# Last batch of an attention and feed-forward kernel: its dense layers by seven block products, with the output feature-major, and a planner with other margins and due times

## The chip, the cores and the metric

One core of a Trainium2 chip runs the whole program. The metric is the device time of one execution in microseconds; three executions of the kernel before gave 443.0, 445.16 and 446.7 us, and their median, 445.16 us, is the time before. Line numbers such as L659 are lines of the kernel before; those of the changed kernel are given as such.

## What is computed

Four batches of 768 tokens, eight heads of 64 features. The first half is an attention in a window of 32 tokens, to which 24 block summaries (maximum of k, mean of v over 32 tokens) are added as further keys. Its output `x` (768 tokens by 512 features a batch) goes through a feed-forward part with a gate. All is float32:

```python
    x_prev = np.concatenate([np.zeros((B, 1, D), dtype=np.float32), x[:, :-1, :]], axis=1)
    xk = mu_k * x + (1.0 - mu_k) * x_prev
    xr = mu_r * x + (1.0 - mu_r) * x_prev
    k = np.maximum(xk @ w_k, 0.0)              # 512 -> 1024
    v = k * k @ w_v                            # 1024 -> 512
    r = 1.0 / (1.0 + np.exp(-(xr @ w_r)))      # 512 -> 512
    return (r * v).astype(np.float32)
```

## The kernel before

**How the work is tiled.** The tokens go through the dense layers in eight halves of 384 tokens (four batches, two halves each; below, half 0 to half 7). For a half there are three blocks of PE work. The gate `gate_tile` (L586) takes three tiles of 128 tokens by 512 features and multiplies by `w_r`. `experts` (L616) runs over eight slices `j` of 128 of the 1024 hidden features: `first(j)` (L621) makes a slice of `k` with features on partitions and 384 tokens wide (L632), ACT squares its positive part (L639, L641), and `second(j)` (L651) multiplies the slice by `w_v` and adds it into three banks of PSUM, tokens on partitions and 512 features wide (L659). DVE multiplies by the gate (L689) and SP stores (L693).

**Precision.** A float32 operand is split into a rounded part (`kh`, `xh`, `w_h`) and its rest (`kl`, `xl`, `w_l`), both in a format that PE takes in one pass. A product is three matmuls: high by high, high by low, low by high. So a `first(j)` is 4 x 3 = 12 matmuls of 128x384, a `second(j)` 9 of 128x512, a gate tile 12 of 128x512. The splits are a cast (L573, L645, L646) and a subtraction (L575, L647) on ACT and DVE. In half 0, where the weights have only just come, the first slices run "plain", on unsplit float32, which PE takes in several passes: `PLAIN = 6, 6` says that six of the eight slices do, in both layers.

**Attention.** A batch has eight units (`unit`, L441): four pairs of heads, two halves of the tokens. A unit goes: scores on PE (L462), mask and row minimum on DVE (L473), exponential on ACT (L477), the factor 1/sum on DVE (L483, L484), normalisation on POOL (L489), a transposition in blocks on DVE (L514, "flip"), four transfers to DRAM ("put", L523) and one back ("get", L527) that finish the transposition, the product with the values on PE (L536), and a copy out of PSUM (L549, L547). The means of v reach the value tile by a transfer that copies them to each window ("spread", L436). All transfers are issued by SP, in one queue.

**What sets the order.** The program is written as a list of operations with costs and due times, and `Plan.schedule` (L145) lays them out: it goes forward in a time of its own, gives each engine the ready operation with the earliest start and due time, and emits the instructions in the order found. Each engine then runs its instructions strictly in that order and waits where data is missing. The table `LENGTH` (L39) has an assumed cost for each operation; a transfer is assumed to take `DMA_FIXED` plus its bytes. `LOCKS` (L70) lists the DVE operations during which the planner keeps POOL idle, and the reverse. Attention of batch b+1 is spread over the two halves before it: unit number n of a batch is due `UNITS` times (7 - n) before the last (L740). The last two halves, 6 and 7, have no attention beside them.

**Buffers.** Forty slots `w` of 128x512 hold the weights: high and low parts of 4 tiles of `w_r`, 8 of `w_k`, 8 of `w_v`.

Of the kernel before, what the change touches and what calls it, by code (L numbers as in the profile page):

```python
# [20 lines left out]
P = 128  # L21
# [23 lines left out]
    norm=345, wcast_p=640, mixa_p=600, kcopy_p=450, evac_a=375, flip=560,  # L45
# [20 lines left out]
ISSUES = dict(put=720, get=400, spread=820)  # L66
# [6 lines left out]
UNITS = 8500  # L73
# [26 lines left out]


class Op:
    def __init__(self, n, ways, due, bufs, size):
        self.n, self.ways, self.due, self.bufs, self.size = n, ways, due, bufs, size
        self.deps, self.succ, self.start, self.finish, self.eng = set(), [], None, None, None


class Plan:
    def __init__(self, pools, later):
        self.pools, self.later, self.ops, self.count = pools, later, [], {p: 0 for p in pools}  # L110
        self.writers, self.readers = {}, {}

    def buf(self, pool, dtype=F32, in_turn=True):
        n = self.count[pool] if in_turn else None
        self.count[pool] += in_turn
        return Buf(pool, n, dtype)
# [28 lines left out]
    def schedule(self):  # L145
# [7 lines left out]
        for o in reversed(self.ops):  # L153
            own = 1.0e9 if o.due is None else o.due
            wait = DMA_FIXED + o.size * DMA_NS_PER_BYTE if "SP" in o.ways else min(c for c, _ in o.ways.values()) + SLACK
            o.due = min([own] + [s.due - wait for s in o.succ])
        waiting = {o: len(o.deps) for o in self.ops}
# [17 lines left out]
        while any(ready.values()):  # L175
            best = None
            for e, now in engines.items():
# [3 lines left out]
                for o, at in ready[e]:  # L181
# [5 lines left out]
                    start, need, ok = max(at, now, o.due - EARLY if e == "SP" and o.name not in ("put", "get") else 0), {}, True  # L187
                    if e == "SP":
                        start = max(start, lanes[-LANES])
                    for x in o.bufs:  # L190
                        if x.place is None:
# [4 lines left out]
                            start = max(start, free_slots[x.pool][k][0])  # L196
# [23 lines left out]
            for x in o.bufs:  # L220
                if x.place is None:
                    _, x.place = free_slots[x.pool].pop(0)
                    turn[x.pool] += x.n is not None
# [16 lines left out]
            for x in o.bufs:  # L240
                x.left -= 1
                if not x.left:
                    end = max(u.finish + LATENCY[u.eng] for u in x.users)
                    pool, places = self.later.get(x.pool, (x.pool, [x.place]))
                    free_slots[pool].extend((end, place) for place in places)
                    free_slots[pool].sort(key=lambda s: s[0])
# [9 lines left out]
def tile_kernel(ctx: ExitStack, tc: tile.TileContext, q, k, vT, v, mask, ident, pool, sel, mu, w_k, w_v, w_r, out):  # L256
# [7 lines left out]
    def slots(name, n, shape):  # L264
# [3 lines left out]
    last_z = Slot(const, "z4", [P, 2, DM], "kt3")  # L268
    pools = dict(
        ktx=[last_kt], w=slots("w", 2 * (NCK + 2 * NCV), [P, 512]),  # L270
        kt=tiles("kt", 3, [P, KL]), qt=tiles("qt", 4, [P, HT]), vx=tiles("vx", 12, [P, S + 1]),
        kg=tiles("kg", 2, [P, 49]), ks=tiles("ks", 2, [P, NS]),
        vs=tiles("vs", 1, [P, NS]), vm=tiles("vm", 3, [P, P]), sp=tiles("sp", 2, [P, P]),
        y=tiles("y", 4, [P, NSL, P]), mn=tiles("mn", 4, [P, NSL]), sm=tiles("sm", 3, [P, 2 * NSL]),
# [564 lines left out]
```

## Time and profile before

| | us |
|---|---|
| runs | 443.0, 445.16, 446.7 |
| the profiled execution, its own time | 446.4 |
| its span, first to last instruction | 444.6 |
| PE busy | 433.3 (97%) |
| DVE busy | 274.5 (62%) |
| ACT busy | 269.1 (61%) |
| POOL busy | 109.4 (25%) |
| mean granted clock of PE | 0.995 |

How to read it: a row of the page or of a view names line, engine, operation, what it writes and reads, how often, and the time. The 1.8 us between the span and the execution's own time lie around the first and last instruction. A busy PE is not PE at its peak: matmuls overlap, so durations of single ones (0.40 us) are longer than the distance from one to the next, and the costs used below are distances between starts. A plain float32 matmul is two records in the trace.

The execution falls into a start of some 44 us, in which inputs arrive and the attention of batch 0 runs; half 0 with the weights arriving (to about 98 us); halves 1 to 5 with the attention of the next batch beside them, about 50 us each (to 354 us); halves 6 and 7 alone (354 to 441 us); and the last stores.

### The profile page before, as it was taken

The page shows a single profiled execution, that of the slowest core. Times are in us where ns is not written, and L with a number is a line of the kernel's source. Part 1 is how long each engine was busy: PE and PEld are TensorE (multiplying, and loading weights), DVE is VectorE, ACT ScalarE, POOL GpSimd, SP SyncE. Part 2 cuts the span into 40 slices and gives each one's busy share as a digit, 9 for nine tenths or more (in the row PEclk, how much of TensorE's full clock was granted, in tenths as well). Part 3 has the DMA queues.
Part 4 walks back from the last instruction along what each step waited for, and adds up shares of the span by engine and source line. Part 5 has one row for each costly group of instructions (what it writes and reads, how often), then busy time and mean ns, then how long its engine had stood idle before and what let it go on. Part 6 is the DMA issues. An engine that isn't in the chain of part 4 may idle for free.

```text
span 444.6 us, 9448 instructions
## 1 busy us (share of the span) xinstructions
PE 433.3 (97%) x3366; PEld 351.4 (79%) x3366; DVE 274.5 (62%) x890; ACT 269.1 (61%) x772; POOL 109.4 (25%) x245
## 2 busy tenths in 40 slices
PE   8998999997999999999999999999999999999996
PEld 8754555685888888887888888887888888888895
DVE  3798999897775658549474649559464444232213
ACT  3699989987855448558665459548665444232220
POOL 0692514672241005132150005232150001000000
PEclk9999999998999999999999999999999999999999
DMA  8968878677767243676647152867642010001001
GB/s 289 404 205 299 300 258 262 210 206 190 255 184 235 103 142 110 192 260 186 164 108 234 41 204 76 267 191 200 189 116 72 1 72 0 0 2 71 1 0 71
DMA packets 41509, 70.82 MB, mean 159 GB/s; under 512 B 4855, under 2 KB 24951, under 8 KB 41463
## 3 DMA queue, kind: packets, MB, share of 16 engines
q1 hardware_dynamic: 41463, 70.23, 49.5%
q8 instruction: 26, 0.43, 0.4%
q14 instruction: 20, 0.16, 0.1%
HBM read 52.71 MB, written 15.73 MB: 154 GB/s over the span
## 4 chain that ended last, share of the span: by engine, by line
PE 80%; DMA 9%; ACT 6%; DVE 3%; issue 1%; SPq 0%; ACTq 0%
PE mm L659 28%; PE mm L632 27%; PE av L536 5%; PE mm L593 4%; PE mm L595 4%; PE mm L594 4%; PE sc L462 4%; DMA st<-in_w_k 2%; ACT y L477 2%; DMA kt<-in_k 2%; PE mm L606 2%; DMA mu_sb<-in_mu 1%; DMA vx<-in_v 1%; DMA qt<-in_q 1%; ACT wc L328 1%
## 5 line engine op out<-in xcount | busy, mean ns | idle before, releaser
L632 PE MATMUL mm<-xs,w 128*128 128x384 f32 x744 | 149.1, 349 | 0.0
L632 PEld LDWEIGHTS mm<-xs,w 128*128 128x128 f32 x744 | 130.8, 188 | 10.5 <-issue 1.9
L489 POOL TENSOR_SCALAR y<-y,rc 128x120 f32<-128x120 f32 x192 | 85.4, 462 | 139.8 <-DVE rc L484 109.7
L659 PE MATMUL mm<-w,kh 128*128 128x512 f32 x348 | 94.6, 400 | 0.4 <-ACT kh L646 0.4
L477 ACT ACTIVATE y<-y,mn 128x120 f32<-128x120 f32 x192 | 73.4, 384 | 19.5 <-DVE mn L473 19.2
L639 ACT ACTIVATE r<-mm 128x384 f32<-128x384 f32 x64 | 31.1, 486 | 88.0 <-PE mm L632 87.9
L659 PEld LDWEIGHTS mm<-w,kh 128*128 128x128 f32 x348 | 64.3, 189 | 13.1 <-ACT kh L646 0.7
L645 DVE CAST kh<-r 128x384 fp32r<-128x384 f32 x41 | 15.4, 375 | 69.8 <-ACT r L641 69.7
L659 PE MATMUL mm<-w,kl 128*128 128x512 f32 x174 | 54.4, 406 | 0.0
L575 DVE TENSOR_TENSOR xs<-xa,xs 128x384 fp32r<-128x384 f32 x56 | 30.2, 554 | 31.2 <-ACT xs L573 31.1
L473 DVE CUSTOM_DVE_ANT_0 y<-sc,mask_sb 128x120 f32<-128x120 f32 x192 | 42.0, 275 | 5.4 <-PE sc L462 5.3
L561 POOL TENSOR_SCALAR xa<-vx,om_sb 128x384 f32<-128x384 f32 x16 | 12.4, 785 | 105.3 <-DVE xs L575 102.2
L659 PEld LDWEIGHTS mm<-w,kl 128*128 128x128 f32 x174 | 31.6, 189 | 7.6 <-DVE kl L647 0.5
L647 DVE TENSOR_TENSOR kl<-r,kh 128x384 fp32r<-128x384 f32 x58 | 32.7, 564 | 7.2 <-ACT kh L646 4.4
L536 PEld LDWEIGHTS av<-pts,vx 120*64 120x64 f32 x768 | 25.1, 138 | 14.4 <-issue 11.2
L477 ACT ACTIVATION_READ_ACCUMULATOR y<-y,mn 128x1 f32 x192 | 36.0, 188 | 0.0
L564 DVE SCALAR_TENSOR_TENSOR xa<-vx,mu_sb,xa 128x384 f32<-128x384 f32 x56 | 33.3, 619 | 2.7 <-ACT xa L558 2.7
L514 DVE STREAM_TRANSPOSE st<-y 128x384 f32<-128x384 f32 x48 | 27.4, 572 | 11.0 <-POOL y L489 7.9
L641 ACT ACTIVATE r<-r 128x384 f32<-128x384 f32 x64 | 33.4, 523 | 1.1
L593 PE MATMUL mm<-w,xs 128*128 128x512 f32 x84 | 33.8, 402 | 0.0
L594 PE MATMUL mm<-w,xs 128*128 128x512 f32 x84 | 33.2, 395 | 0.0
L595 PE MATMUL mm<-w,xs 128*128 128x512 f32 x84 | 33.1, 395 | 0.0
(68 smaller groups left out, 509.4 us busy)
## 6 DMA issues: line engine op xcount, KB each, us to landing
vx<-in_v SPq DMA_DIRECT2D x32, 384.0 KB
far<-st SPq DMA_DIRECT2D x96, 96.0 KB
pts<-far SPq DMA_DIRECT2D x24, 384.0 KB
kt<-in_k SPq DMA_DIRECT2D x15, 544.0 KB
qt<-in_q SPq DMA_DIRECT2D x32, 192.0 KB
out<-z SPq DMA_DIRECT2D x24, 256.0 KB
st<-in_vT SPq DMA_DIRECT2D x12, 384.0 KB
st<-in_w_k SPq DMA_DIRECT2D x8, 512.0 KB
```

Of the source, the lines that this page charges most:

```text
L473: op("DVE", "mask", None, lambda h=h, i=i, var=var: nc.vector.tensor_tensor_reduce(out=y[h].t[:, i, 0:NK], in0=sc[h].t[:, i, 0:NK], in1=ma ...
L477: op("ACT", "exp", None, lambda h=h, i=i: nc.scalar.activation(y[h].t[:, i, 0:NK], y[h].t[:, i, 0:NK], AF.Exp, bias=mn[h].t[:, i:i + 1], s ...
L489: op("POOL", "norm", None, lambda h=h, i=i: nc.gpsimd.tensor_scalar(out=y[h].t[:, i, 0:NK], in0=y[h].t[:, i, 0:NK], scalar1=rc.t[:, NSL * ...
L536: nc.tensor.matmul(av.t[hs, w * QW:(w + 1) * QW], windows(vw)[:, w, hs], pts.t[0:NK, 2 * c:2 * c + 2, h, i], start=True, stop=True,)
L564: op("DVE", "mixd", None, lambda: nc.vector.scalar_tensor_tensor(out=xa.t, in0=xt.t[:, 1 + lo:1 + lo + HT], scalar=mu_sb[:, which, p:p + 1 ...
L593: nc.tensor.matmul(ps.t, xh.t[:, ts], h, start=(p == 0), stop=False)
L594: nc.tensor.matmul(ps.t, xh.t[:, ts], l, start=False, stop=False)
L595: nc.tensor.matmul(ps.t, xl.t[:, ts], h, start=False, stop=(p == NPAIR - 1))
L632: nc.tensor.matmul(ps.t[:, 0:HT], w.t[:, p * P:(p + 1) * P], x[p][s].t, start=(n == 0), stop=(n == len(terms) * NPAIR - 1))
L641: op("ACT", "square", None, lambda: nc.scalar.activation(r.t, r.t, AF.Square), reads=[(r, 0)], writes=[(r, 0)])
L647: op("DVE", "sub", None, lambda: nc.vector.tensor_tensor(out=kl.t, in0=r.t, in1=kh.t.bitcast(F32), op=ALU.subtract), reads=[(r, 0), (kh, 0 ...
L659: nc.tensor.matmul(acc[t].t, a.t[:, t * P:(t + 1) * P], v.bitcast(F32) if single else v, start=start, stop=stop)
```

## The change

The last batch leaves `experts` and has a function of its own, `last_batch`. Its two halves are worked together, and all its results have features on partitions: the output of batch 3 is written to DRAM transposed, and the host turns it back.

- **Gate**: for each half four products of 12 matmuls of 128x384 (L951 of the changed kernel), in place of three tiles of 12 of 128x512.
- **`w_k` and `w_v`**: operand and weight are cut in two by two blocks, and the four output blocks are made from seven block products in place of eight (`seven`): the token side is the two halves, the feature side two halves of the features. Sums and differences of blocks take the place of the eighth product. Those of the weights (T1 to T4, `combine`) are made on DVE from the split weights during the earlier halves, stored to DRAM (16 transfers) and fetched and split again in the last batch (`fetch`). Those of the inputs (s1 to s4) are made in the last batch on DVE or POOL, and split. Block products are kept (`keep`) and added (`add`) on ACT and DVE.
- **Half 0** has five plain slices in place of six.
- **Planner**: `HOLD` adds 900 ns to a transfer's earliest start behind what it waits for, a "put" is assumed to take 460 ns of the queue, not 720, units are due 6.5 us apart, not 8.5, steps of `experts` 4.8 us apart, not 4.4; `EARLY` no longer binds the new stores. The new operations (`comb3`, `comb2`, `tsub`, `sum` and others) have costs in `LENGTH`, and none of them was added to `LOCKS`.
- **Buffers**: when the last user of a pool is placed, its slots pass on to the pools of the last batch (`later`); PSUM banks of the attention become `mm` banks.

```diff
-STEP0 = 5200
-PLAIN = 6, 6
+STEP0 = 5600
+PLAIN = 5, 5
...
-STEP = 4400
-SLACK = 800
+STEP = 4800
+SLACK = 400
...
-GAP = 500
+GAP = 300
...
-ISSUES = dict(put=720, get=400, spread=820)
+ISSUES = dict(put=460, get=400, spread=820)
+HOLD = 900
+AFTER = 130000
...
-UNITS = 8500
+UNITS = 6500
...
-                at = max((d.finish + (0 if d.eng == e and e != "SP" else LATENCY[d.eng]) for d in o.deps), default=0)
+                at = max((o.after, *(d.finish + (HOLD if e == "SP" else 0 if d.eng == e else LATENCY[d.eng]) for d in o.deps)))
...
+    def combine(name, u):
...
+        def t1():
+            tt(tb.f[:, lo], l(b12), l(b11), ALU.subtract)
+            tt(ta.f[:, lo], h(b12), h(b11), ALU.subtract)
+            tt(ta.f[:, lo], ta.f[:, lo], tb.f[:, lo], ALU.add)
+
+        def t2():
+            tt(ta.f[:, hi], h(b22), ta.f[:, lo], ALU.subtract)
+            tt(ta.f[:, hi], ta.f[:, hi], l(b22), ALU.add)
...
+        op("DVE", "comb3", None, t1, reads=reads, writes=[(ta, 0), (tb, 0)]).after = AFTER
+        op("DVE", "comb2", None, t2, reads=[*reads, (ta, 0)], writes=[(ta, 1)])
+        op("DVE", "comb3", None, t3, reads=reads, writes=[(tb, 0), (tb, 1)])
+        op("DVE", "comb2", None, t4, reads=[*reads, (ta, 1)], writes=[(tb, 1)])
...
+    def seven(name, due, x, done):
+
+        nk, nc_ = (4, 2) if name == "wv" else (2, 2 if name == "wr" else 4)
+        got = fetch(name, due - 8000)
...
+        def product(which, a, c, bank, at, first, last):
+            def emit():
+                n = 0
+                for s, w in ((0, 0), (0, 1), (1, 0)):
+                    for k in range(nk):
+                        pair, col = block(which, k, c)
+                        nc.tensor.matmul(bank.t[:, 0:HT], pair[w].t[:, col:col + P], a[k][s].t,
+                                         start=(first and n == 0), stop=(n == 3 * nk - 1), skip_group_check=not first)
+                        n += 1
...
+        a = ready(a11)
+        for c in cs:
+            product("B11", a, c, low[c], n, True, False)
+            u1.append(keep(low[c]))
...
+            product("B21", a, c, bank, n, True, True)
+            add(u1[c], bank)
+            done(0, 0, c, u1[c])
...
+        s1 = total(a21, a22, ALU.add)
+        s2 = total(s1, a11, ALU.subtract)
+        a = ready(s2)
...
+            product("T2", a, c, low[c], n, False, False)
+            u2.append(keep(low[c]))
...
+        s3 = total(a11, a21, ALU.subtract)
...
+            product("T3", a, c, low[c], n, False, False)
+            v.append(keep(low[c]))
...
+        s4 = total(a12, s2, ALU.subtract)
...
-    for n in range(1, 2 * B):
+    for n in range(1, 2 * B - 2):
...
+    last_batch(B - 1)
```

The three places in the built order of which the prediction speaks:

SP's queue at the second unit of batch 1 (around the gate of half 1). `far` is the DRAM tile of a unit, `pts` what comes back of it, `vx<-vm` a spread. Before:

```order
L523 DMA far1_137<-st0_120 32x4x192 x4
L436 DMA vx9_77<-vm2_87 24x6x128
L436 DMA vx1_69<-vm2_87 24x6x128
L445 DMA qt3_67<-in_q 128x384
L436 DMA vx7_75<-vm0_85 24x6x128
L527 DMA pts1_105<-far1_137 128x768
```

In the changed kernel:

```order
L574 DMA far1_100<-st2_0_377 32x4x192 x4
L496 DMA qt3_0_250<-in_q 128x384
L412 DMA vx10_0_353<-in_v 128x768
L574 DMA far2_101<-st0_0_225 32x4x192 x2
L578 DMA pts1_0_372<-far1_100 128x768
```

Before, the unit's "get" (L527) stood behind three spreads; now it stands behind two puts of the next unit.

DVE in the halves that have attention beside them. `kh`, `kl` are the split of a slice of `k`, `st<-y` a flip, `sm`, `rc` the factor 1/sum. Before:

```order
L575 TENSOR_TENSOR xs5_1_1131<-xa2_112,xs4_1_1124 128x384
L647 TENSOR_TENSOR kl0_118<-r0_114,kh0_116 128x384
L514 STREAM_TRANSPOSE st2_122<-y2_92 128x4x96
L514 STREAM_TRANSPOSE st2_122<-y0_90 128x4x96
L377 TENSOR_REDUCE kg0_80<-kt2_63 128x48
```

In the changed kernel, `wc` being the tiles of `combine`:

```order
L774 TENSOR_TENSOR wc0_1_1794<-w16_1_982,w22_0_737 128x256
L774 TENSOR_TENSOR wc0_1_1794<-w20_1_1007,w26_0_764 128x256
L774 TENSOR_TENSOR wc0_1_1794<-wc0_1_1794 128x256
L565 STREAM_TRANSPOSE st1_0_287<-y1_0_114 128x4x96
L565 STREAM_TRANSPOSE st1_0_287<-y3_0_120 128x4x96
L698 TENSOR_TENSOR kl0_0_1124<-r1_0_751,kh0_0_1103 128x384
```

Ten such additions, in four pieces, stand for each of eight pairs of weight tiles: 80 in all, of which 13 stand between the gates of halves 1 and 2, 33 between those of 2 and 3, and 34 between those of 3 and 4.

DVE in the last batch. Before, a half has nothing but this pair again and again, and three products with the gate:

```order
L645 CAST kh0_116<-r0_114 128x384
L647 TENSOR_TENSOR kl0_118<-r0_114,kh0_116 128x384
L645 CAST kh1_117<-r1_115 128x384
L647 TENSOR_TENSOR kl1_119<-r1_115,kh1_117 128x384
L689 TENSOR_TENSOR z3_109<-mm2_132,z3_109 128x512
```

In the changed kernel, where `w_k` ends and `w_v` begins (L970 squares, L832 sums of blocks, L867 keeps a product, L626 makes a low part):

```order
L970 SCALAR_TENSOR_TENSOR xa2n_0_4024<-xa2n_0_4024 128x384
L626 TENSOR_TENSOR vx9n_0_4287<-r1n_0_4391,vx1n_0_4262 128x384
L832 TENSOR_TENSOR vx4n_0_4185<-y3n_0_4183,qt3n_0_4179 128x384
L867 COPY vx7n_0_4107<-bank5_0_259 128x384
L626 TENSOR_TENSOR xs9_0_716<-xa2n_0_4024,vx3n_0_4299 128x384
L832 TENSOR_TENSOR vx6n_0_4295<-vx4n_0_4185,qt0n_0_3955 128x384
L626 TENSOR_TENSOR xs12_0_829<-pts0n_0_4243,vx1n_0_4262 128x384
L626 TENSOR_TENSOR xs15_0_851<-qt2n_0_4158,vx5n_0_4265 128x384
L626 TENSOR_TENSOR kh0n_0_4154<-pts1n_0_4308,xs8_0_661 128x384
L626 TENSOR_TENSOR xs1_1_887<-vx6n_0_4295,kh1n_0_4134 128x384
```

From the first block product of `w_k` on, DVE has 88 instructions: 34 low parts, 18 additions, 10 splits of fetched weights, 9 sums, 5 kept products, 4 squares, 8 products with the gate. PE has 84 + 12 matmuls of the gate and 336 of the block products in one unbroken row.

More of the change, by code (lines that the diff above doesn't have):

```diff
@@ L186, in schedule @@
                         continue
-                    start, need, ok = max(at, now, o.due - EARLY if e == "SP" and o.name not in ("put", "get") else 0), {}, True
+                    start, need, ok = max(at, now, o.due - EARLY if e == "SP" and o.name not in ("put", "get", "far") else 0), {}, True
                     if e == "SP":
@@ new lines, in same, with windows_to @@
+    def same(place):
+        return "mm", [place]
+    wide = []
+    def windows_to(place):
+        wide.append(place)
+        return parts("xf" if len(wide) <= FLOATS else "xs", 2, HT)(place)
+    later = dict(
+        ktx=lambda place: ("z", [Slot(const, "z", None, part=(last_z, n)) for n in range(2)]),
+        kt=parts("w", 2, 512), st=parts("w", 2, 512), we=parts("wf", 1, 512), wc=parts("wf", 1, 512),
+        vx=windows_to, pts=parts("xf", 2, HT), qt=parts("xf", 1, HT), y=parts("xf", 1, HT),
+        xa=parts("xf", 1, HT), r=parts("xf", 1, HT), kh=parts("xs", 1, HT), kl=parts("xs", 1, HT),
+        sc=same, pt=same, av=same,
@@ L282, in tile_kernel @@
     )
     dram = ctx.enter_context(tc.tile_pool(name="dram", bufs=1, space=bass.MemoryType.DRAM))
+    pools["farw"] = tiles("farw", 16, [P, 512], F32, dram)
     pools["far"] = tiles("far", 4, [P, 4, 2 * NSL * 32], pool=dram)
-    plan = Plan(pools, dict(ktx=("z", [Slot(const, "z", None, part=(last_z, n)) for n in range(2)])))
+    plan = Plan(pools, later)
     op, buf = plan.op, plan.buf
@@ new lines, in fetch @@
+    def fetch(name, due):
+        got = {}
+        for u in range(w_f_count[name] // 2):
+            for m in range(2):
+                far = far_w[name, u, m]
+                t, hi, lo = buf("wf", F32, False), buf("w", F32R, False), buf("w", F32R, False)
+                got[u, m] = hi, lo
+                op("SP", "load", due, lambda t=t, far=far: nc.sync.dma_start(out=t.f, in_=far.t),
+                   reads=[(far, 0)], writes=[(t, 0)], size=P * 2048)
+                op("ACT", "tcast", None, lambda t=t, hi=hi: nc.scalar.copy(out=hi.t, in_=t.f), reads=[(t, 0)], writes=[(hi, 0)],
+                   other=("POOL", "wcast_p", lambda t=t, hi=hi: nc.gpsimd.tensor_scalar(
+                       out=hi.t, in0=t.f, scalar1=1.0, scalar2=1.0, op0=ALU.mult, op1=ALU.mult)))
+                op("DVE", "tsub", None, lambda t=t, hi=hi, lo=lo: nc.vector.tensor_tensor(
+                    out=lo.t, in0=t.f, in1=hi.f, op=ALU.subtract), reads=[(t, 0), (hi, 0)], writes=[(lo, 0)])
+        return got
@@ L744, in tile_kernel @@
         experts(b, hf, mixes(b, hf, 0), z)
+    plan.tail = len(plan.ops)
+    last_batch(B - 1)
     order = plan.schedule()
```

265 lines of the change are left out of this document (220 added, 45 removed).

## The prediction

> **What bounds the kernel now.** I read the page first, then the busy time by stage, then who PE waits for.
>
> ```profile
> span 444.6 us, 9448 instructions
> PE 433.3 (97%) x3366; PEld 351.4 (79%) x3366; DVE 274.5 (62%) x890; ACT 269.1 (61%) x772; POOL 109.4 (25%) x245
> PE 80%; DMA 9%; ACT 6%; DVE 3%; issue 1%; SPq 0%; ACTq 0%
> ```
>
> PE is busy for 97% of the span and holds 80% of the chain that ended last (third line). No other engine is over 62%. But these are means, so the stages come next: PE, PE's weight loads, DVE, ACT and POOL, then granted clock and DMA.
>
> ```profile
> core 0: us, PE busy (x) PEld busy (x) DVE busy (x) ACT busy (x) POOL busy (x), PEclk, DMA share, GB/s
> 44.00:82.00 38.00, 37.47 (x256) 20.82 (x256) 35.41 (x116) 35.41 (x101) 14.67 (x29) 1.00 0.79 258
> 82.00:110.00 28.00, 25.24 (x265) 19.50 (x261) 24.32 (x101) 23.46 (x85) 15.74 (x36) 0.94 0.72 210
> 110.00:157.00 47.00, 47.00 (x386) 40.16 (x386) 32.19 (x89) 29.16 (x73) 9.48 (x22) 1.00 0.59 188
> 157.00:207.00 50.00, 50.00 (x421) 41.97 (x419) 33.24 (x120) 30.46 (x99) 12.68 (x30) 1.00 0.56 174
> 207.00:257.00 50.00, 50.00 (x381) 42.54 (x378) 30.05 (x93) 31.41 (x85) 10.79 (x28) 1.00 0.48 146
> 354.40:440.80 86.40, 86.04 (x418) 75.67 (x416) 28.74 (x57) 28.34 (x56) 1.28 (x1) 1.00 0.05 19
> ```
>
> From 110 us on PE has no gap. In the last batch (354.4 to 440.8) it has work for all but 0.4 us while DVE and ACT have 29 of 86 us: a matmul taken out there shortens the kernel, and the other engines have room. Only 82 to 110 shows PE idle, at a lower clock.
>
> ```profile
> PE av L536 <- issue: 2.7, 1, 2.7
> PE mm L606 <- DVE xs L564: 1.4, 1, 1.4
> ```
>
> So PE's own waits are one of 2.7 us, one of 1.4 at the end of the start, and smaller ones. **PE's sum of matmuls is the time, and the change is priced there first.**
>
> **PE's sum.** Distances between starts, from the chain in order of time (first fence) and from PE's timeline (second):
>
> ```profile
> 44.56 2.59 PE mm L632 x8
> 371.74 2.10 PE mm L632 x12
> 373.84 2.10 PE mm L659 x9
> ```
>
> ```profile
> 78.12 2.74 PE L659 MATMUL mm<-w,r 128*128 128x512 f32 x6
> 80.80 0.85 PE L462 MATMUL sc<-kt,qt 64*64 64x120 f32 x24
> 396.80 0.39 PE L593 MATMUL mm<-w,xs 128*128 128x512 f32 x1
> 399.55 0.62 PE L659 MATMUL mm<-w,kh 128*128 128x512 f32 x2
> ```
>
> Twelve matmuls of 128x384 take 2.10 us, nine of 128x512 also 2.10, a gate tile of twelve 399.55 - 396.80 = 2.75. The new products have the form of L632 (a weight block of 128x128 loaded each time, 384 columns moving), so they get its price.
>
> - `w_k`: 16 slices x 2.10 = 33.6 us now. Afterwards 7 x 4 products of 6 matmuls, 28 x 1.05 = 29.4: **-4.2**.
> - `w_v`: 16 x 2.10 = 33.6 now. Afterwards 7 x 2 products of 12, 14 x 2.10 = 29.4: **-4.2**.
> - Gate: 6 x 2.75 = 16.5 now, 8 x 2.10 = 16.8 afterwards: **+0.3**.
> - The sixth slice of half 0, split instead of plain: 2.59 - 2.10 = 0.49 in the first layer and (80.80 - 78.12) - 2.10 = 0.58 in the second: **-1.1**. PE has work on both sides of it, and its two weight tiles must now be split some 7 us sooner, in a stage where DVE has 35.4 of 38 us (44 to 82); if that is late, the 1.1 is not gained.
> - The tail. The last product with the gate is 384 wide, not 512 (0.55 and 0.69 us by rows further down), so **-0.2**; the last store keeps its landing.
>
> ```profile
> 440.49 0.40 PE L659 MATMUL mm<-w,kl 128*128 128x512 f32 x1
> 439.53 2.09 DVE L689 TENSOR_TENSOR z<-mm,z 128x512 f32<-128x512 f32 x3 [1.39 <-PE mm L659]
> ```
>
> Behind PE's last end (440.9) stand 0.7 us of DVE and some 3 us of store, as they will again. Sum so far: -9.4 us.
>
> **The pause at 102 us.** PE's timeline, then SP's queue:
>
> ```profile
> 104.57 1.02 PE L536 MATMUL av<-pts,vx 120*64 120x64 f32 x24 [2.67 <-issue]
> 106.97 0.63 PE L593 MATMUL mm<-w,xs 128*128 128x512 f32 x1
> 108.67 0.40 PE L594 MATMUL mm<-w,xs 128*128 128x512 f32 x1
> ```
>
> ```profile
> 97.74 0.36 SPq L445 DMA_DIRECT2D qt<-in_q  x1
> 99.87 0.80 SPq L436 DMA_DIRECT2D vx<-vm  x1
> 100.84 0.39 SPq L527 DMA_DIRECT2D pts<-far  x1
> ```
>
> The second unit of batch 1 waits for its get: SP sat from 98.1 to 99.87 at a spread whose means ACT had not made, the get behind it was issued at 100.84, and PE went on at 104.57. Then seven matmuls, to 108.67, stood 0.43 apart (the first and last of seven rows), not 2.75/12 = 0.23: another 1.4 us, and the 0.94 of the clock in that stage. The pause costs 2.7 + 1.4 = 4.1 us. The Trainium skill ("TensorE: Matmul & The Clock Gate", section "Why this matters for your kernels") halves the clock after idle gaps of more than about 3 us; here 2.67 us were enough, so by the rule a pause of this size would cost 2.7 and by the trace 4.1, and the trace decides.
>
> In the new order the get no longer stands behind those spreads, but behind two puts of the next unit, which wait for DVE's flips. The gain lies between 0 and 4.1; I take **-2.5**, nearer the upper end, since every transfer there is now planned 0.9 us later than its data.
>
> **DVE and POOL between 110 and 257 us.** This is what the change adds under PE's cover: 80 additions of 128x256. No row has that size; the nearest, by shape, and the product with the gate:
>
> ```profile
> L575 DVE TENSOR_TENSOR xs<-xa,xs 128x384 fp32r<-128x384 f32 x56 | 30.2, 554 | 31.2 <-ACT xs L573 31.1
> L348 DVE TENSOR_TENSOR w<-w,w 128x512 fp32r<-128x512 f32 x19 | 12.8, 682 | 0.6 <-POOL w L346 0.5
> L689 DVE TENSOR_TENSOR z<-mm,z 128x512 f32<-128x512 f32 x24 | 16.3, 691 | 8.2 <-PE mm L659 8.1
> ```
>
> 128 columns more cost 0.13, so 256 columns cost 0.43. Five of the ten in a group need the result just before them; that costs 0.1 each, as in these two rows, where a 0.36 us cast and the subtraction that needs it start 0.46 apart (the row behind them is PE's first use of that cast):
>
> ```profile
> 383.37 0.36 DVE L645 CAST kh<-r 128x384 fp32r<-128x384 f32 x1 [3.18 <-ACT r L641]
> 383.83 0.56 DVE L647 TENSOR_TENSOR kl<-r,kh 128x384 fp32r<-128x384 f32 x1
> ```
>
> ```profile
> 386.30 1.56 PE L659 MATMUL mm<-w,kh 128*128 128x512 f32 x6
> ```
>
> That makes 0.48 each. With 33 of them in half 2, DVE goes from 33.2 to 49.0 of its 50 us; with 34 in half 3 from 30.1 to 46.4. Below: independent instructions overlap, as DVE's timeline shows:
>
> ```profile
> 365.89 1.50 DVE L575 TENSOR_TENSOR xs<-xa,xs 128x384 fp32r<-128x384 f32 x3 [5.80 <-ACT xs L573]
> ```
>
> Three of the 554 ns kind in 1.50 are 0.05 less each, so the true load is nearer 47. Above: 0.68 each, the price of the wider row, makes 55.6 and 53.2, and DVE is the bound by 5.6 + 3.2 = 8.8 us. Between, what is late first is a `kh`: PE takes it at 386.30, 2.6 us after it is made, so one group of three additions (1.4 us) ahead of it on DVE is hidden and two are not quite. I take 0.48 and **+1.5** for the odd late operand, from a range of 0 to 8.8.
>
> POOL's normalisations, six a unit, share something with DVE:
>
> ```profile
> L489 POOL TENSOR_SCALAR y<-y,rc x192: 357/364/1420, 11.7 to 330.9; 128x120 f32<-128x120 f32 x192
> L561 POOL TENSOR_SCALAR xa<-vx,om_sb x16: 579/582/1277, 92.0 to 367.0; 128x384 f32<-128x384 f32 x16
> ```
>
> ```profile
> DVE st L514 <- POOL y L489: 7.9, 12, 1.2
> ```
>
> (Minimum, median, maximum in ns, and DVE's waits.) The same instruction takes 357 or 1420 ns. The "GPSIMD Engine Reference" of the Trainium skill (section "Specifications") says that POOL's access to SBUF is shared with DVE and contended when a DVE instruction has two SBUF inputs, and all 80 additions have two; the spread of the row agrees.
>
> **DVE in the last batch.** Its 88 instructions from the first block product on, at 0.55 each, are 48.4 us beside 58.8 of PE: covered, with 10 to spare. The narrow place is where `w_v` begins. Its third product needs sums over the last output of `w_k`: ACT's positive part and square (two instructions of about 0.5, the second below), two sums, a cast, a subtraction.
>
> ```profile
> L641 ACT ACTIVATE r<-r 128x384 f32<-128x384 f32 x64 | 33.4, 523 | 1.1
> ```
>
> In DVE's order ten instructions stand from that output to the last operand, 10 x 0.55 = 5.5 us, against four products of 2.10 = 8.4 us on PE. It fits, so 0. The 32 transfers of weight sums run while DMA is at 0.5 or less.
>
> **Sum.** -9.4 - 2.5 + 1.5 = -10.4 us. Against the profiled execution's own 446.4 this gives 436.0; that run was 1.2 above the median of the three, so the median goes from 445.2 to **434.8 us**. The own range of this case is 431.7 (all of the pause gained, nothing lost) to 438.4 (nothing of the pause, the 1.1 of the plain slice not gained, 1.5 lost).
>
> **Rivals.**
>
> *The pause only moves.* Units now stand 6.5 us apart, so gets and puts crowd SP in front of each first gate, and one new pause like that at 102 arises while the old one stays: -9.4 + 4.1 = -5.3, 439.9 us. For it: puts that wait for DVE stand ahead of gets. Against: after 110 us the trace has no such pause, with units of the same length.
>
> *The joint between the layers binds.* POOL takes five of the block sums there. At 1.28 us (the longest of L561), not 0.58, they add 3.5 us to 5.5 of DVE and 1.0 of ACT, 10.0 against 8.4: 1.6 us late, and the same again at the later sums: 434.8 + 3.2 = 438.0. Against: the sums for the first three slices can run before `w_k` ends.
>
> *Slower: DVE becomes the bound of halves 2 and 3.* The additions and POOL's normalisations shut each other out, and DVE, in its strict order, stands at flips that wait for POOL. It decides from 0.51 us an addition, where (50 - 33.2) / 33 uses up the room. At 0.73 (0.68 and half of the 0.1 waits) DVE needs 57.3 and 54.9 us: +12.2. Twelve units whose flips wait the longest 1.2 us seen, 14.4 in place of 7.9, add 6.5. 445.2 - 9.4 - 2.5 + 18.7 = 452.0. For it: the mean load is over 90% by my own price, and POOL's spread. Against: overlapping starts, and that the narrower shape should be cheaper than the 0.68 row.
>
> That the change does not do what it says has no place: the built order shows 336 matmuls of 128x384 where there were 192 of 128x384 and 144 of 128x512.
>
> **How the numbers follow.** Forecast 0.64, joint 0.11, pause moved 0.15, DVE bound 0.10. The range runs from 431.0, below the forecast's own end by what single runs scatter, to 443.0, which takes in the first two rivals and part of a DVE loss, and leaves out the last. A measurement tells about 1% (4.5 us) from no change: faster by more means below 440.7. That is the forecast, the joint and about half of the moved pause: 0.82. The rest of the pause and a small part of the DVE case lie within 1%: 0.10. Slower by over 1%: 0.08.
>
> **What would show it.** Right: in the last batch PE without a gap over 0.5 us, 336 products 0.175 apart, about 78 us from its first gate to PE's end (86.4 now, the last products of half 5 among them in both); PE idle between 95 and 110 us under 1 us; DVE at 44 to 49 us in halves 2 and 3; additions at 0.4 to 0.5. Wrong: additions over 0.6, PE waiting for `kl` or for `av`'s get in halves 2 and 3, a stage of 50 us grown by more than 2, or PE waiting for a cast behind the last product of `w_k`.

## The result, and the profile after

The changed kernel takes 430.9 us (median; 428.9 to 432.5) against 445.2 for the kernel before: a ratio of 0.968, 95% interval 0.962 to 0.974, or 14.3 us less. The forecast was 434.8. Its sign and its largest term held; the gain is 3.9 us larger than forecast, and two terms of the sum are off.

The page of the changed kernel, its span, its engines and the chain that ended last:

```profile
span 427.1 us, 9810 instructions
PE 421.6 (99%) x3395; PEld 352.3 (82%) x3395; DVE 340.9 (80%) x1033; ACT 293.7 (69%) x823; POOL 134.0 (31%) x265
PE 92%; DVE 6%; issue 1%; ACT 1%; POOL 0%; DVEq 0%; ACTq 0%; POOLq 0%
```

PE is the bound more purely than before (99% of the span, 92% of the chain), and DVE has gone from 62% to 80%. PE's waits, all of them:

```profile
PE bank L1002 <- POOL zero_sb L997: 1.0, 1, 1.0
PE bank L1002 <- ACT pts L553: 0.6, 1, 0.6
PE bank L855 <- DVE xs L626: 0.4, 1, 0.4
```

The first two lie in the start. The waits of 2.7 us for a unit's get and of 1.4 at the end of the start are gone, and one new wait stands in the block products.

To see where the time came from, both executions are cut at the same points of the program: the first product of half 0, the first product of the gate of half 1, the first of the last batch's gate, PE's end (each is a start, or the last end, in PE's timeline). Before, then after; columns as in the prediction's table by stage:

```profile
44.40:98.07 53.67, 53.05 (x439) 32.91 (x438) 50.58 (x175) 49.10 (x154) 26.15 (x53) 1.00 0.77 248
98.07:354.35 256.28, 253.61 (x2040) 214.25 (x2038) 161.51 (x538) 160.58 (x465) 60.63 (x147) 0.99 0.54 163
354.35:440.89 86.54, 86.18 (x418) 75.72 (x416) 28.88 (x57) 28.39 (x57) 1.28 (x1) 1.00 0.05 19
```

```profile
43.14:93.38 50.24, 50.16 (x437) 32.68 (x435) 49.45 (x187) 49.95 (x156) 28.71 (x55) 1.00 0.77 257
93.38:345.02 251.64, 251.64 (x2043) 213.17 (x2041) 190.64 (x612) 166.23 (x470) 63.45 (x146) 1.00 0.60 189
345.02:423.82 78.80, 78.25 (x442) 76.90 (x440) 67.60 (x119) 46.37 (x99) 21.99 (x23) 1.00 0.21 69
```

| stage | before | after | difference |
|---|---|---|---|
| start, to the first product of half 0 | 44.40 | 43.14 | -1.3 |
| half 0, to the gate of half 1 | 53.67 | 50.24 | -3.4 |
| halves 1 to 5, to the last batch | 256.28 | 251.64 | -4.6 |
| last batch | 86.54 | 78.80 | -7.7 |

These are 17.1 us and not 14.3, because this profiled execution of the changed kernel is its fastest (428.9) and that of before one of its slower ones (446.4). The last batch grew shorter by 7.7, as its matmul counts say. In halves 1 to 5 PE's busy time fell by 2.0 and its idle time of 2.7 vanished, though DVE did 29 us more there (161.5 to 190.6). One thing the waits do not show: where the plan foresees a gap on PE it puts matmuls of zeros there (L715, in the changed kernel L1002), which count as busy. Between the first product of half 0 and the gate of half 2 there were six of them before (0.8 us), and there are none now.

### The profile page after: what moved, and what is told of

Its sections match the earlier page's. It is cut to its first block, busy times and chain, and to the rows that moved or that the text cites. A ratio compares the mean times of both kernels' runs of the same rounds, so it can differ in the third digit from the quotient of the medians.

```text
span 427.1 us, 9810 instructions
## 1 busy us (share of the span) xinstructions
PE 421.6 (99%) x3395; PEld 352.3 (82%) x3395; DVE 340.9 (80%) x1033; ACT 293.7 (69%) x823; POOL 134.0 (31%) x265
## 4 chain that ended last, share of the span: by engine, by line
PE 92%; DVE 6%; issue 1%; ACT 1%; POOL 0%; DVEq 0%; ACTq 0%; POOLq 0%
PE bank L710 25%; PE bank L683 24%; PE bank L855 10%; PE bank L587 6%; PE bank L513 6%; PE bank L951 4%; PE bank L644 3%; PE bank L646 3%; PE bank L645 3%; PE bank L1002 3%; PE bank L547 2%; PE bank L657 1%; DVE xs L626 1%; DVE xs L615 1%; PE bank L446 1%
## 5 line engine op out<-in xcount | busy, mean ns | idle before, releaser
L683 PE MATMUL bank<-xs,w 128*128 128x384 f32 x556 | 112.7, 351 | 0.0
L683 PEld LDWEIGHTS bank<-xs,w 128*128 128x128 f32 x556 | 97.6, 188 | 8.6 <-issue 0.8
L710 PE MATMUL bank<-w,kh 128*128 128x512 f32 x258 | 70.5, 401 | 0.0
L710 PEld LDWEIGHTS bank<-w,kh 128*128 128x128 f32 x258 | 46.6, 188 | 9.3 <-issue 0.6
L524 DVE CUSTOM_DVE_ANT_0 y<-bank,mask_sb 128x120 f32<-128x120 f32 x192 | 42.6, 274 | 10.1 <-PE bank L513 10.0
L710 PE MATMUL bank<-w,kl 128*128 128x512 f32 x129 | 39.8, 401 | 0.0
L587 PEld LDWEIGHTS bank<-pts,vx 120*64 120x64 f32 x768 | 25.2, 137 | 10.9 <-issue 6.0
L565 DVE STREAM_TRANSPOSE st<-y 128x384 f32<-128x384 f32 x48 | 26.8, 567 | 6.4 <-POOL y L540 6.3
L855 PE MATMUL bank<-xs,w 128*128 128x384 f32 x130 | 31.4, 337 | 0.4 <-DVE xs L626 0.4
L587 PE MATMUL bank<-pts,vx 120*64 120x64 f32 x768 | 29.7, 226 | 0.0
L710 PEld LDWEIGHTS bank<-w,kl 128*128 128x128 f32 x129 | 23.4, 188 | 6.0 <-issue 0.8
L513 PE MATMUL bank<-kt,qt 64*64 64x120 f32 x768 | 27.4, 271 | 0.0
L626 DVE TENSOR_TENSOR xs<-xa,xs 128x384 fp32r<-128x384 f32 x40 | 21.5, 549 | 6.4 <-ACT xs L624 6.4
L855 PEld LDWEIGHTS bank<-xs,w 128*128 128x128 f32 x130 | 23.3, 188 | 0.7 <-DVE xs L626 0.7
```

Source lines behind the costliest of these rows:

```text
L513: nc.tensor.matmul(cells(sc[h])[cs, i, 0:NK], qt.t[hs, n * QW:(n + 1) * QW], kt.t[hs, w * KB:w * KB + NK], start=True, stop=True,)
L524: op("DVE", "mask", None, lambda h=h, i=i, var=var: nc.vector.tensor_tensor_reduce(out=cells(y[h])[:, i, 0:NK], in0=cells(sc[h])[:, i, 0:N ...
L565: op("DVE", "flip", due - AHEAD + 8000 + 600 * h, lambda h=h: nc.vector.transpose(out=turned()[:, :, h], in_=cells(y[h]).rearrange("p i (r ...
L587: nc.tensor.matmul(av.t[hs, w * QW:(w + 1) * QW], windows(vw)[:, w, hs], weights_of(pts)[0:NK, 2 * c:2 * c + 2, h, i], start=True, stop=True,)
L626: op("DVE", "sub", None, lambda: nc.vector.tensor_tensor(out=xl.t, in0=xa.f, in1=xh.f, op=ALU.subtract), reads=[(xa, 0), (xh, 0)], writes= ...
L683: nc.tensor.matmul(ps.t[:, 0:HT], w.t[:, p * P:(p + 1) * P], x[p][s].t, start=(n == 0), stop=(n == len(terms) * NPAIR - 1))
```

## The experiments

Each was timed in five rounds beside the kernel before (445.4, 446.2 and 446.1 us in the three groups), and its ratio is to that. By their intervals, 0.3 to 0.6% to each side, a difference between two of these runs is uncertain by some 2 us. In the text, a time above or below the changed kernel is against its 430.9.

**Old planner, new last batch.**

```diff
-STEP0 = 5600
-PLAIN = 5, 5
-STEP = 4800
-SLACK = 400
-GAP = 300
-ISSUES = dict(put=460, get=400, spread=820)
-HOLD = 900
-UNITS = 6500
+STEP0 = 5200
+PLAIN = 6, 6
+STEP = 4400
+SLACK = 800
+GAP = 500
+ISSUES = dict(put=720, get=400, spread=820)
+HOLD = 0
+UNITS = 8500
```

> The changed kernel with all eight planner and plain-slice constants of before (PLAIN 6, UNITS 8500, STEP 4400, SLACK 800, GAP 500, put 720, HOLD 0, STEP0 5200). Theory: the last batch gives 8 us by itself and the other 5 to 6 us come from the start, the pause near the first gate and the plain slice, which stand with the old constants; in its SP order two spreads stand before the second get of batch 1 again. So 437 us (436 to 439), PE waiting 2 to 3 us for that get, and a last batch of about 79 us. Rival: the constants hardly matter and the products give nearly all: 431 to 433.

Measured 436.5 us, ratio 0.980 (0.976 to 0.985). PE's waits between 90 and 130 us in its trace:

```profile
PE bank L587 <- ACT y L528: 1.7, 1, 1.7
PE bank L587 <- ACT r L690: 0.7, 1, 0.7
PE bank L587 <- DVE xs L626: 0.7, 1, 0.7
```

Three waits of the products with the values (L587), 3.1 us together, where the changed kernel has none. The 1.7 stands at the second unit of batch 1, whose get went out at 99.92 with PE going on at 103.16: it may be the expected wait for that get, though the view names ACT. So the last batch alone gives 8.9 us of the 14.3, and the constants the rest.

**New planner, old last batch.**

```diff
-    for name in ("wk", "wv"):
-        for u in range(w_f_count[name] // 2):
-            combine(name, u)
...
-    for n in range(1, 2 * B - 2):
+    for n in range(1, 2 * B):
...
-    last_batch(B - 1)
```

> The changed kernel with its new constants, but the last batch by the old route (token-major, eight slices, no sums of weights). Theory: the additions under PE cost nothing, so only the last batch is lost: 430.9 + 7.9 = 438.8 us (437.5 to 440), with a last batch of 86.5 us and no pause near the first gate. Rival: the 80 additions on DVE cost some 1.5 us that come back here: 437 or less.

Measured 439.2 us, ratio 0.986 (0.983 to 0.990): as the theory has it. The constants alone give 6.2 us. 8.9 and 6.2 are 15.1, close to the 14.3 of both: the two parts hardly disturb each other.

**Eight block products.** Layout, gate and planner stay; `seven` makes each of the four output blocks from two block products, eight in all, and no sums of blocks are made.

```diff
-        a = ready(a11)
-        u1 = []
...
+        a = {(r, s): ready(x[r, s]) for r in range(2) for s in range(2)}
+        for r in range(2):
+            for s in range(2):
+                for c in cs:
+                    bank = buf("mm")
+                    product(f"B1{s + 1}", a[r, 0], c, bank, n, True, False)
+                    product(f"B2{s + 1}", a[r, 1], c, bank, n + 1, False, True)
+                    done(r, s, c, bank)
+                    n += 2
```

> The changed kernel with feature-major output and gate as they are, but the layers of the last batch by eight block products, and no sums of weights. Theory: 4 x 6 + 2 x 12 more matmuls of 128x384 twice over, two layers of 4.2 us, so 430.9 + 8.4 - 0.4 (the one wait for a low part) = 438.9 us (437.5 to 440); the layout itself gives or takes nothing. Rival: the sums, keeps and additions of the seven-product scheme cost some of its gain, 436 or less here.

Measured 439.1 us, ratio 0.986 (0.983 to 0.989), 8.2 above the changed kernel. One of its six executions took 839.7 us, for a reason that the record does not show; the median of the other five is 438.9. It equals the old last batch within 0.3: the feature-major layout by itself is worth nothing that this measurement can show, and the seven-product scheme is worth its matmuls, one layer's 4.2 twice over, less 0.2 to 0.4.

**The get ahead of the spreads, in the kernel before.** The prediction laid the pause at 102 us on the queue: the get stood behind three spreads, one of which SP had to wait for. This kernel takes only that away.

```diff
     order = plan.schedule()
+    g = [i for i, o in enumerate(order) if o.name == "get"][1]
+    p = [i for i, o in enumerate(order[:g]) if o.name == "put"][-1]
+    late = [o for o in order[p:g] if o.name == "spread" and o.eng == "SP"]
+    order = order[:p] + [o for o in order[p:g] if o not in late] + [order[g]] + late + order[g + 1:]
```

> The kernel before with one change: in SP's queue the get of the second unit of batch 1 stands ahead of the three spreads that were between its puts and it; every other engine's order is as before. Theory: the pause at 102 us and the half clock behind it were this queue position: PE's wait of 2.7 falls to under 0.5 and the time by 3 to 4 us, to 441.5 (441 to 443). Rival: the spreads are late then and the next unit waits for them, 445.

Measured 447.2 us, ratio 1.005 (1.002 to 1.009): slower, so the theory fell. PE's waits from 98 to 130 us, and SP's queue at this place:

```profile
PE av L536 <- DMA pts<-far: 2.0, 2, 1.3
PE av L536 <- issue: 1.4, 1, 1.4
```

```profile
95.82 2.23 SPq L523 DMA_DIRECT2D far<-st  x4
102.54 0.34 SPq L527 DMA_DIRECT2D pts<-far  x1
102.97 2.49 SPq L436 DMA_DIRECT2D vx<-vm  x3
```

The get now waits in the queue itself until its puts have landed (102.54, against the last put's issue that ended at 98.05), and everything behind it starts later. The one pause of 2.7 became three of 3.4 in all, two of them at later units. So the queue position was a part of the pause: at the second unit it fell from 2.7 to 1.3 us, and the half clock behind it is gone. The rest was the time that the unit's puts took to land, and waits of 1.4 and 0.7 us are new behind it. What held the spread in the kernel before is not certain either. ACT had made its means by 97.92 us, before SP came to the spread at 98.1; SP's waits from 98 to 100 us name a load that was issued at 92.46, and exponentials on ACT:

```profile
SPq L436 <- DMA st<-in_vT: 1.7, 1, 1.7
SPq L436 <- ACT y L477: 0.7, 1, 0.7
```

From the gate of half 1 to the last batch this execution took 255.7 us, against 256.3; its start was 3.4 us longer than in the trace of before, in the same order, so the profile does not say why the kernel is slower by 0.5%, only that the 3 to 4 us did not come.

**One constant at a time, in the changed kernel.** HOLD first.

```diff
-HOLD = 900
+HOLD = 0
```

> The changed kernel with HOLD = 0 in place of 900, all else as it is. Theory: the margin behind each transfer's data is what took the stalls near the first gate away; without it the second get of batch 1 stands behind two spreads again, PE waits there 2 to 3 us and some more at later units, and the time is 434 to 436. Rival: the shorter spacing of the units did it, and HOLD is worth nothing: 431 (430 to 432).

Measured 443.6 us, ratio 0.995 (0.992 to 0.998): 12.7 above the changed kernel, far beyond what either theory gave, so nearly the whole gain is gone. The wait of 2 to 3 us that the theory set at the second get did not come (from 95 to 130 us PE waits 0.7 us for a get and 0.8 for other things). The loss stands in two places. From the first product of half 0 to the gate of half 2 this execution takes 112.7 us, against 102.6 in the changed kernel. PE's waits there are 3.1 us; most of the rest is inside its busy time, as matmuls of zeros that the plan put into gaps it foresaw, where the changed kernel has none:

```profile
L1002 PE MATMUL bank<-zero_sb 128*128 128x128 f32 x42 | 5.9, 280 | 0.4 <-ACT vm L478 0.4
```

And its stages from gate to gate of halves 2 and 3 are 54.1 and 54.0 us (50.7 and 48.9 in the changed kernel, shown below), with PE idle for 2.7 and 3.2 of them and the clock at 0.97 in the second:

```profile
153.45:207.59 54.14, 51.40 (x383) 42.81 (x382) 45.94 (x148) 31.30 (x91) 13.83 (x28) 1.00 0.66 212
207.59:261.58 53.99, 50.78 (x416) 42.44 (x414) 37.01 (x121) 33.82 (x95) 15.27 (x34) 0.97 0.52 160
```

What SP's queue waits for between 44 and 345 us, the row of the gets, in the changed kernel and then without HOLD:

```profile
SPq L578 <- DMA far<-st: 19.1, 18, 4.6
```

```profile
SPq L578 <- DMA far<-st: 32.9, 40, 3.0
```

Without the margin the planner issues gets whose puts have not landed; SP stands at 40 of them instead of 18 (19 times, 14.4 us, in the kernel before, which has no margin either but looser units), and what is queued behind comes late: PE waits for spreads (`vx<-vm`, 2.3 us) and gets (1.3 us) in halves 1 to 5. It also waits 3.7 us there for `kh`, `kl` and `r`, operands of DVE and ACT; that the queue made these late too is not shown.

```diff
-UNITS = 6500
+UNITS = 8500
```

> The changed kernel with UNITS = 8500 in place of 6500. Theory (the margin HOLD did it): the stalls stay away, 431 (430 to 432), though two spreads stand ahead of the second get here too. Rival: units due earlier are late under the spreads, and the pause comes back, 434 to 436.

Measured 434.6 us, ratio 0.975 (0.970 to 0.979): 3.7 lost. So the spacing counts as well. With 8500 the first unit is due 14 us earlier, but it is not half 0 that suffers (50.1 us, against 50.2): in the trace the start is 2.1 us longer and halves 1 to 5 are 4.6 longer, with 2.4 us of PE's waits in them. The second get stands behind two spreads again, as expected (they start at 93.82, the get at 96.21), and PE waits 0.2 us for that unit, which speaks against the queue position as the whole cause.

```diff
-ISSUES = dict(put=460, get=400, spread=820)
+ISSUES = dict(put=720, get=400, spread=820)
```

> The changed kernel with a put assumed to hold the queue 720 ns, not 460. The second get of batch 1 stands behind puts as in the changed kernel, ahead of the spreads. Theory: no pause, 431 (430 to 432.5). Rival: the queue is then planned too full, and units slip: 433 or more.

Measured 430.9 us, ratio 0.967 (0.962 to 0.971): no difference.

```diff
-PLAIN = 5, 5
+PLAIN = 6, 6
```

> The changed kernel with six plain slices in half 0, not five. Theory: two plain blocks of 2.59 in place of two split ones of 2.10, PE without a gap: 430.9 + 1.1 = 432.0, and up to 2 more if the pause returns, since two spreads stand ahead of the second get in this order. Rival: the later splits take weight off DVE and ACT in the start, 430.9 or less.

Measured 431.0 us, ratio 0.967 (0.962 to 0.972): no difference that this measurement can show, where 1.1 was expected. In its trace one spread (88.46 us) stands between the second unit's puts and its get (91.87), and PE's only wait behind the start is 0.9 us, put down to ACT.

**Old constants with HOLD alone.** The old planner of the first experiment, but with `HOLD = 900` left in.

> The changed kernel with the planner and plain-slice constants of before, but HOLD = 900 kept. Theory: the margin behind a transfer's data is what takes the stalls near the first gate away, with any spacing of the units: 431 to 433. Rival: HOLD is needed only where units are packed 6.5 us apart, and nothing changes against 0 with the old constants: 436 to 438.

Measured 434.2 us, ratio 0.972 (0.969 to 0.975): between the two. HOLD is worth 2.3 us with the old constants (3.7 by the ratios, since the two runs were timed in different groups) and 12.7 with the new. Seen from the other side, the other new constants lose 7.1 us without the margin (436.5 to 443.6) and gain 3.3 with it (434.2 to 430.9). Which of them needs the margin was not tried: the spacing was varied only with it, and `STEP`, `STEP0`, `SLACK` and `GAP` not alone.

**Fewer and more additions.** The same order on every engine, with four additions in a group of ten, then with each written twice.

```diff
         def t1():
             tt(tb.f[:, lo], l(b12), l(b11), ALU.subtract)
-            tt(ta.f[:, lo], h(b12), h(b11), ALU.subtract)
-            tt(ta.f[:, lo], ta.f[:, lo], tb.f[:, lo], ALU.add)
...
         def t2():
             tt(ta.f[:, hi], h(b22), ta.f[:, lo], ALU.subtract)
-            tt(ta.f[:, hi], ta.f[:, hi], l(b22), ALU.add)
```

> The changed kernel, every engine's order as it is, but of the ten additions in each group of weight sums only four are left (32 in all, not 80); the sums T1 to T4 lack the other parts, so the output of the last batch is another one. Theory: the additions lie wholly under PE, 430.9 (430 to 432). Rival (the forecast's 1.5 us for late operands, from 80 additions): 430 or less, 0.9 gained.

Measured 431.4 us, ratio 0.967 (0.964 to 0.970): no gain from 48 additions less that this measurement can show; the 0.9 of the rival is below what it can tell.

```diff
         def t2():
             tt(ta.f[:, hi], h(b22), ta.f[:, lo], ALU.subtract)
             tt(ta.f[:, hi], ta.f[:, hi], l(b22), ALU.add)
+            tt(ta.f[:, hi], h(b22), ta.f[:, lo], ALU.subtract)
+            tt(ta.f[:, hi], ta.f[:, hi], l(b22), ALU.add)
```

> The changed kernel, every engine's order as it is, but each group's additions written twice (160 in all); repeated accumulations make the output of the last batch another one. At 0.41 each, DVE would have 55 of 50 us to do in half 2 and 52 in half 3. Theory: DVE's room is then used up and the surplus, 5.2 + 2.0 us, comes through: 436 to 438. Rival: operands have so much lead that the surplus is worked off in the next half: under 433. The rival of the prediction, additions that shut POOL out and are bound already with 80, would give 445 and more.

Measured 457.7 us, ratio 1.024 (1.021 to 1.027): 26.8 above the changed kernel for 80 additions more, which are 80 x 0.41 = 33 us of DVE. Halves 2 and 3 from gate to gate, in the changed kernel and then with doubled additions (DVE is the third engine):

```profile
145.77:196.50 50.73, 50.73 (x383) 42.89 (x382) 46.05 (x156) 34.07 (x102) 11.54 (x29) 1.00 0.67 217
196.50:245.37 48.87, 48.87 (x415) 41.48 (x414) 40.16 (x123) 32.08 (x89) 13.26 (x27) 1.00 0.61 185
```

```profile
147.83:213.23 65.40, 56.55 (x383) 46.76 (x382) 61.21 (x195) 34.38 (x102) 12.57 (x29) 0.92 0.56 187
213.23:272.34 59.11, 51.35 (x415) 42.31 (x414) 54.81 (x158) 32.65 (x91) 14.05 (x27) 0.97 0.48 144
```

In both doubled halves the stage has grown until DVE's work fits in (65.40 and 59.11): DVE is idle for 4.2 to 4.3 us and is then the bound. The expected 7 us took 55 and 52 us of DVE work in stretches of 50 us. From gate to gate the work is 61.2 and 54.8 us, 10.5 and 5.9 more than these stages last in the changed kernel; that is 16.4 of the 24.9 us by which they grew. The rest is time that DVE did not fill. Half 2 in three stretches shows where:

```profile
147.83:177.83 30.00, 25.96 (x142) 21.57 (x140) 29.28 (x79) 17.68 (x40) 4.07 (x8) 1.00 0.47 165
177.83:187.83 10.00, 8.38 (x53) 7.32 (x54) 7.32 (x28) 3.67 (x15) 0.96 (x3) 0.83 0.61 186
187.83:213.23 25.40, 22.21 (x189) 17.88 (x189) 24.61 (x90) 13.04 (x49) 7.53 (x19) 0.87 0.65 213
```

In the first and the last DVE is 97 to 98% busy. In the second it waits 2.4 us for scores from PE. PE had itself waited 2.8 us for a `kl` just before, and its next twelve products of 128x384 took 3.3 us, not 2.1. So a late operand costs PE the pause and some time at a lower clock, and then holds up DVE in turn. In half 2 of the changed kernel DVE has 4.7 us free; at how many additions between 80 and 160 it begins to bind was not measured. PE's longest waits of this stretch name the operands that come late:

```profile
PE bank L710 <- DVE kh L696: 6.5, 3, 3.1
PE bank L710 <- DVE kl L698: 6.0, 3, 2.8
```

They are the `kh` and `kl` of which the prediction spoke. The kernel was not planned anew with the doubled cost, so a better order of 160 additions was not tried.

**The gate by seven products as well.** A version that might beat both.

```diff
-    for name in ("wk", "wv"):
+    for name in ("wr", "wk", "wv"):
         for u in range(w_f_count[name] // 2):
             combine(name, u)
...
+        took_r = seven("wr", start, xr, gated)
```

> The changed kernel with the gate of the last batch by seven block products too: 14 products of 6 matmuls in place of 8 of 12, 14.7 us of PE in place of 16.8; 20 more additions of weights, four more tiles stored and fetched. Theory: PE stays without a gap, 430.9 - 2.1 = 428.8 (427.8 to 430). Rival: the sums of the gate's inputs follow the last attention unit at once and PE waits for them, 431 or more.

Measured 433.1 us, ratio 0.970 (0.968 to 0.973): no gain, and the interval leaves open whether it is a loss. Its last batch, then PE's longest wait in it and two in the halves before:

```profile
350.24:429.32 79.08, 77.43 (x430) 74.66 (x428) 73.77 (x132) 52.69 (x116) 21.79 (x21) 1.00 0.23 72
```

```profile
PE bank L855 <- DVE vx5n L626: 0.8, 1, 0.8
PE bank L587 <- DMA far<-st: 2.3, 1, 2.3
PE bank L587 <- DMA pts<-far: 1.6, 1, 1.6
```

The last batch is no shorter than the 78.8 of the changed kernel, though it has 12 matmuls less. PE is idle in it for 1.7 us (0.6 in the changed kernel), most of that waiting for DVE, and its busy time fell by 0.8 only. DVE is full: up to 420 us it is busy for 68.9 of 69.8 us. The profiled execution (434.4 us) loses its time before that: it reaches the last batch at 350.2 us, 5.2 later than the changed kernel's, and 3.9 of these are two waits for a unit's transfers, at 99.1 and 310.7 us. Whether the added sums and stores brought these waits or the new plan did is open.

## Why the prediction was right, and where it was not

**The matmuls (-8.3 of the -9.4): right.** -4.2 for each layer, +0.3 for the gate and -0.2 in the tail stand against 8.9 by the old planner and 8.2 by eight block products; in the trace the last batch went from 86.5 to 78.8 us, where about 78 were forecast. The forecast that 0 would be lost at the joint of the two layers missed by little: one wait of 0.4 for a low part.

**The sixth plain slice (-1.1): not found.** Six slices took 431.0 and five 430.9. What hides it stays open: each of the two orders is another plan with pauses of its own.

**The pause (-2.5): too small, and its cause held only in part.** This is the step that failed. The trace showed a get behind spreads, and the prediction took the queue position for the cause and the new position for the cure. The pause did go: halves 1 to 5 lost 4.6 us in the trace, where the prediction had priced the pause with its half clock at 4.1 and taken 2.5. But with the get put ahead of the spreads the kernel before grew slower, as its pause was only halved and new ones came at later units; and with two spreads ahead of the get again (units 8.5 us apart) PE waited 0.2 us. Nor had ACT still to make the spread's means when SP came to it. What works is the planner's margin together with the other new constants: as a whole they give 5.6 to 6.2 us by the two experiments at the head; in the changed kernel HOLD is worth 12.7 and the spacing 3.7. The prediction mentioned the margin in half a sentence and gave it no term. It also looked for the gain at one pause only. The start grew shorter by 1.3 us, and half 0 by 3.4, where the forecast had 1.1; PE's idle time there fell from 0.6 to 0.1, and the six matmuls of zeros are gone.

**The additions (+1.5): 0.** The size came out at the price of the narrower shape, below the 0.48 assumed:

```profile
L774 DVE TENSOR_TENSOR wc<-w,w x16: 415/418/427, 131.3 to 237.1; 128x256 f32<-128x256 f32 x16
L774 DVE TENSOR_TENSOR wc<-wc,w x16: 424/426/527, 137.5 to 239.3; 128x256 f32<-128x256 f32 x16
L540 POOL TENSOR_SCALAR y<-y,rc x192: 357/365/1363, 12.6 to 321.9; 128x120 f32<-128x120 f32 x192
```

None took longer than 0.53 us, and POOL's normalisations kept their spread (365 and 1363 now, 364 and 1420 before). DVE was busy for 46.1 of 50.7 us in half 2 and 40.2 of 48.9 in half 3, inside or below the 44 to 49 forecast. PE has no idle time in halves 1 to 5, so no operand was late enough to stop it, and four in ten of the additions cost as much as all ten within what the timing can tell.

**The rivals.** DVE as the bound did not happen with 80 additions. With 160 it did, through late `kh` and `kl` and not, as the rival had it, through flips that wait for POOL: in the doubled halves DVE's waits name PE, ACT and a store. The price of 0.51 an addition at which the rival decides was not reached (0.42). The moved pause is what one finds when only the queue order is changed. The condition of the joint came true and its price did not: POOL's eight sums there took 1.0 to 1.3 us each, not 0.58, and the joint cost 0.4, not 3.2.

**The sum by measured terms:** -8.3 for the last batch, some -6 for the constants, 0 for the additions, -14.3 together; the forecast had -8.3, -3.6 and +1.5. Both errors point the same way, so neither hid the other.

**What stays open.** A single execution can still show the pause. In the run with fewer additions, whose order is that of the changed kernel, the profiled execution (434.1 us, the slowest of its six, 430.8 to 434.1) has it at 99.8 us:

```profile
99.83 0.92 PE L587 MATMUL bank<-pts,vx 120*64 120x64 f32 x24 [2.07 <-DMA pts<-far]
101.53 0.63 PE L644 MATMUL bank<-w,xs 128*128 128x512 f32 x1
101.95 0.63 PE L645 MATMUL bank<-w,xs 128*128 128x512 f32 x1
105.13 0.40 PE L644 MATMUL bank<-w,xs 128*128 128x512 f32 x1
105.36 0.39 PE L645 MATMUL bank<-w,xs 128*128 128x512 f32 x1
```

How often such a pause comes, the granted clock of each execution tells, since half clock behind a pause lowers it. It was 0.998 or less in 39 of the 45 executions of the kernel before that were timed beside the experiments, and in 21 of 30 of the three other kernels without the margin (old planner, HOLD = 0, the get ahead of the spreads). In the kernels with the margin, doubled additions aside, it was so in 5 of 52. In the kernel before, the six executions above 0.998 have a median of 443.4 us and the others one of 446.1. So the margin makes such pauses rarer, and a part of the scatter between executions is their coming and going. Pauses that leave the clock full are not in this count.

## What to carry to other kernels

Where transfers are issued in one queue in program order, give the planner a margin behind each transfer's data before packing them closer: the margin was worth several times more with the tight constants (12.7 us) than with the loose ones (2.3 to 3.7), and moving one transfer ahead of others halved its wait and left new ones behind it. Where the program fills foreseen gaps with matmuls of zeros, count those as waits too. Work added to an engine beside the bound is free while that engine has room, here up to 91% of a stage with 80 additions; far beyond it is paid almost in full, and late operands then slow the bound itself. Read the room stage by stage, not from the mean of the span, and not as a fixed share: in half 0 of the changed kernel DVE is busy for 49.5 of 50.2 us and PE is idle for 0.1. And a saving of matmuls by additions on another engine (seven products for eight) pays only while that engine has the room: it did for two layers, and with the third the last batch, with DVE full, got no shorter.

## What the runs showed of the hardware

**DVE and POOL slow each other down.** In the last batch, where `w_k` ends, POOL makes sums of two tiles. DVE's timeline of the changed kernel, then POOL's:

```profile
387.61 0.55 DVE L626 TENSOR_TENSOR xs<-r0n,xs 128x384 fp32r<-128x384 f32 x1
393.10 1.38 DVE L626 TENSOR_TENSOR xs<-xa1n,xs 128x384 fp32r<-128x384 f32 x1
394.40 0.55 DVE L871 TENSOR_TENSOR xa2n<-bank,xa2n 128x384 f32<-128x384 f32 x1
396.98 1.37 DVE L626 TENSOR_TENSOR vx9n<-r1n,vx1n 128x384 fp32r<-128x384 f32 x1
399.21 0.54 DVE L626 TENSOR_TENSOR xs<-xa2n,vx3n 128x384 fp32r<-128x384 f32 x1
```

```profile
392.72 1.34 POOL L832 TENSOR_TENSOR vx0n<-vx2n,qt1n 128x384 f32<-128x384 f32 x1
394.14 1.21 POOL L832 TENSOR_TENSOR pts1n<-vx0n,pts1n 128x384 f32<-128x384 f32 x1
396.60 1.33 POOL L832 TENSOR_TENSOR pts1n<-xa1n,qt2n 128x384 f32<-128x384 f32 x1
```

The same subtraction takes 0.55 us alone and 1.38 beside a POOL sum; POOL's own sum took 1.01 us at 385.62, with DVE adding from PSUM beside it, and 1.34 at 392.72. The addition at 394.40, one of whose inputs is a PSUM bank, keeps its 0.55 though POOL works beside it. That is the sharing of which the prediction spoke, and the trace agrees with the "GPSIMD Engine Reference" of the Trainium skill (section "Specifications") in this too, that two SBUF inputs on DVE make the contention. PE's only wait in this batch is the 0.4 us at 399.8, for a low part that stood behind these in DVE's order.

**Half clock after a pause.** After the 2.07 us pause above, the gate's matmuls stand 0.42 apart, then 0.23, as they did after the 2.67 of before. After one of 1.91 at 227.5 us, without HOLD, six matmuls of 128x512 took 2.1 us and not 1.5. After a pause of 2.33 at 310.7 us, in the run with the gate by seven products, PE goes on at full clock: the twelve products of 128x384 behind it take 313.87 - 311.58 = 2.29 us, where half the clock would make it 4.2:

```profile
310.74 0.92 PE L587 MATMUL bank<-pts,vx 120*64 120x64 f32 x24 [2.33 <-DMA far<-st]
311.58 2.35 PE L683 MATMUL bank<-xs,w 128*128 128x384 f32 x12
313.87 0.85 PE L513 MATMUL bank<-kt,qt 64*64 64x120 f32 x24
```

So a pause of 1.9 to 2.7 us may or may not cost more than itself (another 1.4 us in the kernel before); its length alone does not decide.
